# Loading and transposing the first batch by pairs of neighbouring tokens, with products in place of transposes

## The chip, the cores and the metric

The kernel runs on one core of one Trainium2 chip. The metric is device time in microseconds (us) of one execution of the whole program. Engines are named as in the profile: PE is TensorE (the matrix engine), PEld its weight loads, DVE is VectorE, ACT is ScalarE, POOL is GpSimd, SP is SyncE. SP and ACT each own a DMA queue (in the profile, q1 is SP's and q10 is ACT's), and both queues are served by the same 16 DMA engines.

## The reference

Two blocks are computed, one after the other, on B = 8 batches, H = 8 heads, S = 512 tokens of D = 64 values a head, and Ns = 32 state rows a head:

```
scores = x @ state^T / 8            # (8, 8, 512, 32), softmax over the 32 state rows
xread  = softmax(scores) @ state    # tokens read the state
scores2 = state @ x^T / 8           # softmax over the 512 tokens
sread  = softmax(scores2) @ x       # states read the tokens
rows   = concat(xread, sread) per batch, heads side by side   # (8*544, 512)
h = rows @ w_in ; g = h * erf(softplus(h)) ; out = g @ w_out    # d_ff = 2048
```

The output is (4352, 512) in float32. The weights arrive as 8-byte floats and are converted on the chip by ACT and DVE.

## The kernel before

The second block is 99% of what PE does. Batches 1 to 7 and the state rows go through a Strassen-like scheme of seven products (`hidden7`, `project7`, `store7`; L543 and L650 in the profile). Batch 0 is different: it runs while the weights are still being fetched and converted, with plain products (`first0` L764, `some0`/`project` L600), and its order is written out by hand from `first0(0, 0, g0[0])` on. `in_order` pins that order on PE, DVE, ACT and SP, so an instruction that waits holds up everything behind it on its engine.

The change touches the beginning of batch 0. These are its steps, in order:

- **Loads.** `x_t[0]` is one tile of 128 partitions x (4 chunks, 8 heads, 64 values). Chunk c holds tokens 128c to 128c+127, one token a partition. The four chunks are four DMAs (L112) of 256 KB each, in runs of 64 floats (256 bytes); chunks 0 and 2 go on ACT's queue, 1 and 3 on SP's. Before them each queue carries half of the state of batch 0 (32 KB, L109); behind them SP's queue carries the first weights (L138).
- **`attention0`** works in two halves of two chunks each. `turn(t)` transposes the half (L315): for each chunk (order 1, 0 and then 2, 3) and each pair of heads, one PE transpose of 128 tokens x 128 values into PSUM. `copies(t, xp)` moves the result to SBUF, half of it on ACT (L320) and half on DVE (L321). `score(t)` multiplies by the state (L328). Then come 32x32 block transposes of the scores on DVE (L334), the softmax (`exps`: L342 maximum and L343 difference on DVE, L344 exponential on ACT; `sum_` L347), and `normalise`. In program order: half 0 is turned and copied, the state of batch 0 is transposed (L182, copied by L183), a filler product runs (`warm`, L169), half 0 is scored, half 1 is turned, copied and scored.
- **Later users.** `read_tokens(0, ...)` (L277) multiplies the token softmax by `x_t[0]` some 88 us in, and `put_x(0, ...)` (L675) stores the four tiles of output rows of batch 0.

`warm(n)` issues products of the identity that nobody reads. In the profile one float32 product of the program stands as two PE records, and a transpose as one: the opening `warm(8)` is 16 records, the eight transposes of `turn(0)` are eight.

Of the kernel before, what the change touches and what calls it, by code (L numbers as in the profile page):

```python
# [8 lines left out]
F32 = mybir.dt.float32  # L9
# [7 lines left out]
def kernel(  # L17
# [17 lines left out]
    nc = tc.nc  # L35
    B, H, S, D = x.shape
    Ns = state.shape[2]
    d_model, d_ff = moe_w_in.shape
    P = 128
    NI = H // 2  # L40
    NC = S // P
# [4 lines left out]
    TB = S + Ns  # L46
# [5 lines left out]
    xin = ctx.enter_context(tc.tile_pool(name="xin", bufs=1))  # L52
# [10 lines left out]
    ident = const.tile([P, P], F32, name="ident")  # L63
    make_identity(nc, ident)

    x_t = {}


    def load_x(b):
        t = xin.tile([P, NC, H, D], F32, name="x")  # L70
        for h in range(H):
            nc.sync.dma_start(out=t[:, :, h, :], in_=x[b, h].rearrange("(c p) d -> p c d", p=P))
        x_t[b] = t
# [30 lines left out]


    st = const.tile([P, B, P], F32, name="st")
    x_t[0] = xin.tile([P, NC, H, D], F32, name="x")
    for e in range(2):
        (nc.scalar, nc.sync)[e].dma_start(out=st[:, 0, D * e:D * e + D],  # L109
                                      in_=state[0].rearrange("(i e) n d -> e i n d", e=2)[e])  # L110
    for c in range(NC):
        (nc.scalar, nc.sync)[c % 2].dma_start(  # L112
            out=x_t[0][:, c], in_=x[0, :, P * c:P * c + P].rearrange("h p d -> p h d"))

    def load_st():
        for h in range(H):
# [49 lines left out]
    def warm(n):  # L166

        for _ in range(n):
            last = nc.tensor.matmul(out=spare[:, 0:P], lhsT=ident, rhs=ident, start=True,  # L169
                                    stop=True)  # L170
        return last
# [5 lines left out]
    def states(bs, pool=ps_at, name="at"):  # L177


        ps = pool.tile([P, len(bs), P], F32, name=name)  # L180
        for k, b in enumerate(bs):
            last = nc.tensor.transpose(out=ps[:, k], in_=st[:, b, :], identity=ident)  # L182
        nc.scalar.copy(st[:, bs[0]:bs[-1] + 1, :], ps)  # L183
        return last
# [46 lines left out]
    def normalise(a, z1):  # L231
        nc.vector.tensor_scalar(z1, z1, 1e-9, None, op0=ALU.add)
        nc.vector.reciprocal(z1, z1)
        for e in range(2):
            nc.vector.tensor_tensor(a[:, e], a[:, e], over(z1[:, e]), op=ALU.mult)

    def largest(sc):
        m2 = small.tile([P, 2], F32, name="m2")
        for e in range(2):
            nc.vector.reduce_max(out=m2[:, e:e + 1], in_=sc[:, e], axis=AX.X)  # L240
        nc.vector.tensor_scalar(m2, m2, -scale, None, op0=ALU.mult)
        return m2

    def weigh_tokens(sc, m2, a2):

        z2 = small.tile([P, 2], F32, name="z2")
        for e in range(2):
            nc.scalar.activation(out=a2[:, e], in_=sc[:, e], func=ACTF.Exp, bias=m2[:, e:e + 1],
                                 scale=scale, accum_out=z2[:, e:e + 1])
        return z2  # L250

    def inverse(z):
        nc.vector.tensor_scalar(z, z, 1e-9, None, op0=ALU.add)
        nc.vector.reciprocal(z, z)

    def turn_weights(a2):
        a2T = att.tile([P, 2, NC, P], F32, name="sc")
        for e in range(2):
            ps = ps_at.tile([P, NC, P], F32, name="at")
            for c in range(NC):  # L260
                nc.tensor.transpose(out=ps[:, c, :], in_=a2[:, e, P * c:P * c + P],
                                    identity=ident)
            nc.scalar.copy(a2T[:, e], ps)
        return a2T
# [3 lines left out]
    def read_tokens(b, a2T, z2, pool=ps_at, name="at"):  # L268


        xt = x_t.pop(b)
        sr = pool.tile([P, 2, D], F32, name=name)
        for e in range(2):
            for c in range(NC):
                for i in reversed(range(NI)):
                    q = slice(Ns * i, Ns * i + Ns)
                    nc.tensor.matmul(out=sr[q, e, :], lhsT=a2T[:, e, c, q],  # L277
                                     rhs=xt[:, c, 2 * i + e, :],
                                     start=(c == 0), stop=(c == NC - 1))
        sn = sn_t[b] = const.tile([P, 2, D], F32, name="sn0") if b == 0 else \  # L280
            st[:, b - 1, :].rearrange("p (e d) -> p e d", e=2)
        for e in range(2):
            nc.vector.tensor_scalar(sn[:, e], sr[:, e], z2[:, e:e + 1], None, op0=ALU.mult)
# [8 lines left out]
    def attention0(between):  # L292

        H2 = S // 2
        NB = NC * NI // 2
        xt = x_t[0]
        xT = xin.tile([P, NI, S // Ns, Ns], F32, name="xq").rearrange("p i m n -> p i (m n)")
        both = att.tile([P, NI, S], F32, name="xT")  # L300
        sc = att.tile([P, 2, S], F32, name="sc")
        aT[0] = keep.tile([P, 2, S], F32, name="aT")
        a = both[:, 0:2].rearrange("p e (k n) -> p e k n", n=Ns)
        m1, z1 = (small.tile([P, 2, NC * NI], F32, name=n) for n in ("m1", "z1"))
        cols = [slice(H2 * t, H2 * t + H2) for t in range(2)]
        blocks = [slice(NB * t, NB * t + NB) for t in range(2)]
        over = lambda v: v.unsqueeze(3).to_broadcast([P, 2, NB, Ns])

        def turn(t):
            xp = [ps_o.tile([P, 2, H2], F32, name="o%d" % (2 * t)),  # L310
                  ps_h.tile([P, 2, H2], F32, name="h") if t else
                  ps_o.tile([P, 2, H2], F32, name="o1")]
            for c in ((1, 0), (2, 3))[t]:
                for i in range(NI):
                    nc.tensor.transpose(out=xp[i // 2][:, i % 2, P * (c % 2):P * (c % 2) + P],  # L315
                                        in_=xt[:, c, 2 * i:2 * i + 2, :], identity=ident)
            return xp

        def copies(t, xp):
            nc.scalar.copy(xT[:, 0:2, cols[t]], xp[0])  # L320
            nc.vector.tensor_copy(xT[:, 2:4, cols[t]], xp[1])  # L321

        def score(t):
            s2 = [ps_at.tile([P, S], F32, name="at")[:, 0:H2] for _ in range(2)]
            for i in range(NI):
                for e in range(2):
                    r, q = slice(D * e, D * e + D), slice(Ns * i, Ns * i + Ns)
                    nc.tensor.matmul(out=s2[e][q, :], lhsT=st[r, 0, q], rhs=xT[r, i, cols[t]],  # L328
                                     start=True, stop=True)
            return s2  # L330

        def turn_scores(t, s2):
            for e in range(2):
                nc.vector.transpose(out=both[:, e, cols[t]], in_=s2[e])  # L334

        def copy_scores(t, s2):
            for e in range(2):
                nc.scalar.copy(sc[:, e, cols[t]], s2[e])

        def exps(t):  # L340
            k = blocks[t]
            nc.vector.reduce_max(out=m1[:, :, k], in_=a[:, :, k], axis=AX.X)  # L342
            nc.vector.tensor_tensor(a[:, :, k], a[:, :, k], over(m1[:, :, k]), op=ALU.subtract)  # L343
            nc.scalar.activation(out=a[:, :, k], in_=a[:, :, k], func=ACTF.Exp, scale=scale)  # L344

        def sum_(t):
            nc.vector.reduce_sum(out=z1[:, :, blocks[t]], in_=a[:, :, blocks[t]], axis=AX.X)  # L347

        copies(0, turn(0))
        states(range(1), ps_h, "h")  # L350
        warm(1)
        s0 = score(0)
        xp = turn(1)
        turn_scores(0, s0)
        copy_scores(0, s0)
        copies(1, xp)
        warm(3)
        s1 = score(1)
        exps(0)
        between[0]()  # L360
        turn_scores(1, s1)
        exps(1)
        between[1]()
        copy_scores(1, s1)
        sum_(0)
        between[2]()
        sum_(1)
        between[3]()
        normalise(a, z1)
        for e in range(2):  # L370
            nc.vector.transpose(out=aT[0][:, e], in_=both[:, e])

        def rest():
            a2 = both[:, 2:4]
            m2 = largest(sc)
            yield
            z2 = weigh_tokens(sc, m2, a2)
            inverse(z2)
            yield
            a2T = turn_weights(a2)  # L380
            yield
            read_tokens(0, a2T, z2)
            yield

        return rest()
# [9 lines left out]
    def attention(b, xT=None):  # L395
# [40 lines left out]
        if b + 1 < B:  # L436
            load_x(b + 1)
# [231 lines left out]
        put(0, o1, slice(E2, d_model))  # L669

    def put_x(b, h):
        rows = out[TB * b:TB * b + S].rearrange("(c p) e -> c p e", p=P)

        def go(r, ot, c=slice(0, d_model)):
            nc.sync.dma_start(out=rows[2 * h + r][:, c], in_=ot[:, c])  # L675
        return go
# [388 lines left out]
```

## Time and profile before

| | us |
|---|---|
| median of 4 runs | 732.46 (731.81 to 732.93) |
| the profiled execution, whole | 732.70 |
| its span, first to last instruction | 730.9 |
| outside the span | 1.8 |
| PE busy in the span | 722.5 |
| DVE busy | 524.5 |
| ACT busy | 395.8 |
| start of the first transpose of batch 0 | 6.06 |
| end of the last transpose of batch 0 | 11.36 |
| first product of the second block (L764) | 22.4 |

A row of the timeline gives start, duration, engine, line, operation, output and inputs, shape, and how many; in brackets stands the idle time before it and what ended that. The chain of waits is followed back from the last instruction: each piece has a start, the time it adds to the chain, and what ran. A PE record's duration includes the time in which the result drains, so records overlap; what one costs in a row of many is read from the distance of their starts, or from the chain.

### The profile page before, as it was taken

What the parts mean: (1) busy time and instruction counts of PE and PEld (TensorE: products, weight loads), DVE (VectorE), ACT (ScalarE), POOL (GpSimd) and SP (SyncE); (2) the same over time, 40 slices, a digit from 0 to 9 for tenths busy, and PEclk for the clock granted to TensorE, in tenths of its full rate; (3) what the DMA queues carried; (4) which work ended last, traced back from release to release, by engine and by line L of the source; (5) the groups of instructions that cost most, each with busy time, mean ns of one, the idle gap of its engine ahead of it and who ended that gap; (6) DMA issues with size and microseconds to landing.
All of it is one profiled execution on the core that took longest, in us unless ns stands there. A gap on an engine that the chain in (4) does not pass through costs nothing.

```text
span 730.9 us, 12161 instructions
## 1 busy us (share of the span) xinstructions
PE 722.5 (99%) x5032; PEld 588.3 (80%) x5032; DVE 524.5 (72%) x768; ACT 395.8 (54%) x500; POOL 0.7 (0%) x6
## 2 busy tenths in 40 slices
PE   8999999999999999999999999999999999999998
PEld 7434435889889888988989888988898899999996
DVE  4988887997798677867587669866686656674423
ACT  4898894665556444754455445544575434443340
POOL 0000000000000000000000000000000000000000
PEclk9999999999999999999999999999999999999999
DMA  7577842330152103310061104220111000000001
GB/s 234 172 209 249 224 93 58 87 60 30 19 103 65 48 1 65 81 30 30 1 145 25 34 1 96 57 52 2 42 47 30 30 1 30 1 30 1 30 1 29
DMA packets 139166, 46.40 MB, mean 63 GB/s; under 512 B 126696, under 2 KB 130536, under 8 KB 139112
## 3 DMA queue, kind: packets, MB, share of 16 engines
q1 hardware_dynamic: 136708, 44.88, 24.4%
q10 hardware_dynamic: 2404, 0.75, 0.5%
q8 instruction: 39, 0.64, 0.4%
q14 instruction: 15, 0.12, 0.1%
HBM read 33.03 MB, written 8.91 MB: 57 GB/s over the span
## 4 chain that ended last, share of the span: by engine, by line
PE 90%; ACT 5%; DVE 3%; issue 1%; DMA 1%; SPq 0%; DVEq 0%; ACTq 0%
PE o L650 49%; PE h L543 27%; PE o L600 5%; PE at L457 2%; PE h L764 1%; PE h L457 1%; PE at L197 1%; ACT raw L146 1%; PE at L471 1%; ACT L774 1%; DMA x<-in_x_dram 1%; PE h L277 1%; ACT s L774 1%; ACT w_in L144 0%; PE at L277 0%
## 5 line engine op out<-in xcount | busy, mean ns | idle before, releaser
L650 PE MATMUL o<-w_out,s 128*128 128x256 f32 x480 | 118.0, 380 | 0.0
L650 PE MATMUL o<-raw,hs 128*128 128x256 f32 x480 | 117.3, 382 | 0.0
L550 ACT ACTIVATE s<-hs 128x512 f32<-128x512 f32 x120 | 75.3, 629 | 74.3 <-DVE hs L551 74.0
L650 PE MATMUL o<-w_out,hs 128*128 128x256 f32 x480 | 114.1, 380 | 0.0
L650 PEld LDWEIGHTS o<-raw,hs 128*128 128x128 f32 x480 | 89.9, 190 | 22.6 <-issue 10.9
L551 DVE TENSOR_TENSOR hs<-hs,h 128x512 f32<-128x512 f32 x90 | 61.8, 687 | 62.5 <-PE h L543 62.4
L650 PEld LDWEIGHTS o<-w_out,hs 128*128 128x128 f32 x480 | 90.8, 190 | 16.3 <-issue 4.2
L650 PEld LDWEIGHTS o<-w_out,s 128*128 128x128 f32 x480 | 84.6, 191 | 7.9
L551 DVE TENSOR_TENSOR hs<-s,h 128x512 f32<-128x512 f32 x60 | 41.0, 684 | 67.4 <-PE h L543 67.0
L543 PEld LDWEIGHTS h<-aT,m 128*128 128x128 f32 x672 | 83.8, 192 | 4.3 <-issue 1.4
L543 PE MATMUL h<-aT,m 128*128 128x128 f32 x672 | 84.4, 275 | 0.0
L595 DVE TENSOR_TENSOR s<-s,hs 128x2048 f32<-128x2048 f32 (+1 forms) x31 | 68.7, 2218 | 20.4 <-ACT s L593 20.4
L554 ACT COPY s<-h 128x512 f32<-128x512 f32 x29 | 17.0, 585 | 107.7 <-PE h L543 107.7
L600 PE MATMUL o<-w_out,s 128*128 128x512 f32 x128 | 59.1, 600 | 0.6 <-DVE s L777 0.5
L543 PE MATMUL h<-sy,sx 128*128 128x128 f32 x448 | 59.4, 275 | 0.0
L543 PEld LDWEIGHTS h<-sy,sx 128*128 128x128 f32 x448 | 56.7, 192 | 2.0 <-issue 0.5
L593 ACT ACTIVATE s<-s 128x2048 f32<-128x2048 f32 x30 | 57.4, 1912 | 0.3
L559 ACT COPY hs<-h 128x512 f32<-128x512 f32 x29 | 16.9, 584 | 74.8 <-PE h L543 74.8
L650 PE MATMUL o<-raw,s 128*128 128x256 f32 x240 | 56.8, 379 | 0.0
L600 PEld LDWEIGHTS o<-w_out,s 128*128 128x128 f32 x128 | 23.1, 190 | 31.1 <-issue 25.8
L650 PEld LDWEIGHTS o<-raw,s 128*128 128x128 f32 x240 | 43.5, 190 | 4.7
L550 ACT ACT_TABLE_LOAD x31 | 39.8, 1283 | 0.5
(139 smaller groups left out, 917.1 us busy)
## 6 DMA issues: line engine op xcount, KB each, us to landing
raw<-in_moe_w_in_dram SPq DMA_DIRECT2D x8, 1024.0 KB, 5.3
raw<-in_moe_w_out_dram SPq DMA_DIRECT2D x8, 1024.0 KB, 4.7
xq<-in_x_dram SPq DMA_DIRECT2D x112, 64.0 KB, 2.1
x<-in_x_dram SPq DMA_DIRECT2D x56, 128.0 KB, 2.7
out_dram<-ot SPq DMA_DIRECT2D x18, 256.0 KB, 2.0
sc<-xT SPq DMA_DIRECT2D x112, 32.0 KB, 1.9
out_dram<-ot SPq DMA_DIRECT2D x28, 128.0 KB, 1.7
x<-in_x_dram SPq DMA_DIRECT2D x2, 256.0 KB, 5.3
```

The costliest lines, as they stand in the source:

```text
L146: lambda: nc.scalar.activation(out=lo, in_=lo, func=ACTF.Copy, scale=2.0 ** -29)], \
L457: nc.tensor.matmul(out=ps[k][e][q, :], lhsT=st[r, b, q], rhs=w_in[r, 2 * g:2 * g + 2, i, :], start=True, stop=True)
L543: last = nc.tensor.matmul(out=bank[:, q], lhsT=lhsT, rhs=rhs, start=(first and i == 0 and k == 0), stop=(i == GF - 1 and k == len(ops) - 1 ...
L550: nc.scalar.activation(out=s[:, k], in_=hs[:, k], func=ACTF.Softplus)
L551: add = lambda o, x, y: nc.vector.tensor_tensor(o, x, y, op=ALU.add)
L554: copy(m1, p)
L559: copy(c11, p)
L593: nc.scalar.activation(out=s, in_=s, func=ACTF.Erf)
L595: nc.vector.tensor_tensor(s[:, k], s[:, k], hs[:, k], op=ALU.mult)
L600: nc.tensor.matmul(out=acc[r], lhsT=gT[:, i, P * r:P * r + P], rhs=w_out[:, GF * g + i, :], start=(g == 0 and i == 0), stop=(g == NG - 1 a ...
L650: nc.tensor.matmul(out=acc[bank][:, E2 * c:E2 * c + E2], lhsT=lhs[:, i, :], rhs=rhs[:, g, i, :], start=(first and i == 0 and c == 0), stop ...
L774: nc.scalar.activation(out=gT[0][:, ks], in_=gT[0][:, ks], func=ACTF.Erf)
```

## The change

The tile of `x` of batch 0 gets the order (heads, chunks, values) in each partition, and "chunk" c of partition p now means token 4p + c. The load is again four DMAs of 256 KB: half t (chunks 2t and 2t + 1, that is two neighbouring tokens of each partition) and four heads each. Two neighbouring tokens of a head lie side by side in memory, so a run is now 512 bytes. ACT's queue carries heads 0 to 3 of both halves, SP's heads 4 to 7. `turn` no longer issues a transpose for a pair of heads but two products with the identity, one for a head: 128 tokens x 64 values as the stationary operand, 128 columns of the identity moving, into partitions 0 to 63 or 64 to 127 of the same PSUM region. `put_x(0, ...)` stores row 4p + c of the output from partition p of tile c. Everything else, the order of the other instructions on all engines included, is as before.

```diff
-    x_t[0] = xin.tile([P, NC, H, D], F32, name="x")
+    x_t[0] = xin.tile([P, H, NC, D], F32, name="x").rearrange("p h c d -> p c h d")
...
-    for c in range(NC):
-        (nc.scalar, nc.sync)[c % 2].dma_start(
-            out=x_t[0][:, c], in_=x[0, :, P * c:P * c + P].rearrange("h p d -> p h d"))
+    for t in range(2):
+        for k in range(2):
+            c, h = slice(2 * t, 2 * t + 2), slice(4 * k, 4 * k + 4)
+            (nc.scalar, nc.sync)[k].dma_start(
+                out=x_t[0][:, c, h].rearrange("p c h d -> p h c d"),
+                in_=x[0, h].rearrange("h (p c) d -> p h c d", c=NC)[:, :, c])
...
             for c in ((1, 0), (2, 3))[t]:
                 for i in range(NI):
-                    nc.tensor.transpose(out=xp[i // 2][:, i % 2, P * (c % 2):P * (c % 2) + P],
-                                        in_=xt[:, c, 2 * i:2 * i + 2, :], identity=ident)
+                    for e in range(2):
+                        nc.tensor.matmul(
+                            out=xp[i // 2][D * e:D * e + D, i % 2, P * (c % 2):P * (c % 2) + P],
+                            lhsT=xt[:, c, 2 * i + e, :], rhs=ident, start=True, stop=True)
...
-        rows = out[TB * b:TB * b + S].rearrange("(c p) e -> c p e", p=P)
+        rows = out[TB * b:TB * b + S].rearrange("(p c) e -> c p e" if b == 0 else
+                                                "(c p) e -> c p e", p=P)
```

## The prediction

> **What bounds the kernel now.** I read the page first, for what bounds the whole:
>
> ```profile
> span 730.9 us, 12161 instructions
> PE 722.5 (99%) x5032; PEld 588.3 (80%) x5032; DVE 524.5 (72%) x768; ACT 395.8 (54%) x500; POOL 0.7 (0%) x6
> ```
>
> PE is at work nearly always, but in the opening much of that is filler. So I read the chain of waits over the first 60 us:
>
> ```profile
> 1.54 4.47 DMA x<-in_x_dram
> 6.02 0.04 issue
> 6.06 2.22 PE o L315 x8
> 8.28 0.21 PE h L182
> 8.49 0.43 PE o L169 x2
> 8.92 1.22 PE at L328 x16
> 10.14 0.55 PE o L315 x2
> 10.69 0.22 PE h L315 x2
> 10.91 0.22 PE o L315 x2
> 11.12 0.23 PE h L315 x2
> 11.36 0.02 issue
> 11.38 0.69 DVE xq L321
> 12.07 0.60 DVE m L342
> ...
> 15.56 0.63 ACT xT L344
> ...
> 22.57 3.47 PE h L764 x8
> ```
>
> Every piece that the change touches is on the chain: the load of x, both turns (L315), the score of half 0 between them (L328), and the DVE copy behind the last transpose (L321). From there it goes through DVE, ACT and PE to the end, and the load of x is the only DMA on it. Later work waits for computation and not for a clock of its own, so I take a shift of the copy at 11.38 to reach the end in full.
>
> Third, the timeline, for what a turn waits for and costs, and for a product with column groups:
>
> ```profile
> 1.35 3.78 PE L169 MATMUL o<-ident 128*128 128x128 f32 x16 [1.35 <-POOL ident masks.py:199]
> 6.06 2.22 PE L315 MATMUL o<-ident,x 128*128 128x128 f32 x8 [0.93 <-DMA x<-in_x_dram]
> 7.16 0.72 PEld L315 LDWEIGHTS o<-ident,x 128*128 128x128 f32 x4 [0.38 <-DMA x<-in_x_dram]
> 87.63 1.10 PE L277 MATMUL at<-x,sc 128*32 128x64 f32 x64
> ```
>
> `warm(8)` is 16 records, two for a float32 product; the eight transposes of half 0 are eight, one each. PE waits twice: until 6.06 for chunk 1 (SP's queue), until 7.16 for chunk 0 (ACT's). L277's 32 products go to four groups of 32 columns, and its 64 records take 1.03 us of the chain.
>
> Fourth, the DMA view, asked for 4 to 5, 6 to 7 and 10 to 12 us:
>
> ```profile
> DMA packets 1139, 0.29 MB, mean 288 GB/s; under 512 B 1139, under 2 KB 1139, under 8 KB 1139
> DMA packets 857, 0.22 MB, mean 217 GB/s; under 512 B 857, under 2 KB 857, under 8 KB 857
> DMA packets 416, 0.82 MB, mean 410 GB/s; under 512 B 16, under 2 KB 16, under 8 KB 416
> ```
>
> With 256-byte packets (x) both queues together move 217 to 288 GB/s; with 2 KB packets (weights) 410.
>
> **The change part by part.** A difference of 0.2% (1.46 us) is about what a measurement of this kernel tells from none.
>
> *Loads.* The first product now needs ACT's DMA, the later one, and the other 15 stand behind it; half 0 starts when both DMAs have landed. ACT's packets of x start in number near 3.85 us (53 between 3.8 and 4.0, 28 in the 0.4 us before). The landing at 7.16 is 3.3 us later, of which 1.1 lie behind the last packet (SP's chunk 1: last packet near 4.95, PE released at 6.06). So 2.2 us are transfer. The trace has no 512-byte packets. By the packet time of 16 engines, 256 B at 217 GB/s is 18.9 ns and 2 KB at 410 GB/s is 79.9 ns; on the line between them 512 B is 27.6 ns, or 297 GB/s, 1.37 times the rate. 2.2 / 1.37 = 1.6, so the landing is at 3.85 + 1.6 + 1.1 = 6.55: **-0.6 us**. Ends: no faster (7.16); the full 410/217 = 1.89 times, with 0.3 us less to issue since half as many packets are described: 5.8. I take the line because 512 is far nearer to 256 than to 2048.
>
> The Trainium skill, "DMA: Bandwidth & Descriptors", Specifications, puts the smallest transfer for line rate at 512 B and the fabric's ceiling at 435 GB/s. By it 2.2 us would become 2.2 x 217 / 435 = 1.1 and the landing 6.05, half a microsecond better than my line; no row here shows it.
>
> *Turn of half 0.* Eight transposes become 16 products, 32 records of 128 columns. Before the clock of PE rises a record costs 0.22 us (four transposes from 7.16 to about 8.04). One after the other that is 7.0 us; with two column groups at once 3.5. L277 shows such groups at work: 64 records of 64 columns in 1.03 us are 16.1 ns each, and 64 columns alone would cost 55.7 ns by the 0.111 us of 128 columns (L543: 16 records in 1.78 us), so 3.46 run at once where 4 could. For two groups that is 1.73 to 2; records twice as long carry less overhead, and I take 1.9: 3.7 us. Behind the landing of the second DMA there were four transposes, 0.9 us. So **+2.8 us**, ends +2.6 and +6.1. PE reaches 10.25, and with the same 0.25 us of drain the DVE copy of half 0 starts near 10.5 instead of 8.3.
>
> *Behind it.* L182, L183 and the filler keep their 0.64 us, and the score starts near 11.15. The records of L315 fall from 0.22 to 0.11 us apart at about 10.5; I take it that PE's clock rises at the same time after the change. Then the score of half 0 runs at the pace that half 1 has now (0.82 us against 1.22): **-0.4 us**, end +0.2 if the clock rises later.
>
> The Trainium skill, "TensorE: Matmul & The Clock Gate", Part 1, has PE at half clock until a window of about 3.4 us was busy, with windows that run free. It agrees with the step from 0.22 to 0.11; its windows could fall differently in another run, which would move the sum by some tenths.
>
> *Turn of half 1.* Its data has long landed. 32 records at 0.111 / 1.9 are 1.87 us, with 0.1 of drain 1.95, against 1.22 (10.14 to 11.36): **+0.7 us**, ends +0.65 and +2.4.
>
> The same page's Terms call the transpose mode four times as fast for FP32. Here warm() and L315 show two records against one, so a factor of two; by the page half 1 would be 3.7 us and the sum about 5 us worse. The rows decide.
>
> *At nothing.* The DVE block transposes of the scores of half 0 stay ahead of the copy of half 1 and end well before it (10.97 against 11.38 now). Weight loads are of 64 columns and run beside the other group's products, as L277's do (0.94 us of loads within 1.03); if they did not, the turns would be the serial ones below. The stores at about 130 us keep 2 KB packets and counts; only the next user of `ot` would wait, and a store lands in 2.2 us. L277 reads 64 floats in a row as before. Weights follow x on SP's queue and come earlier, but ACT takes the first of them at 13.96 behind its own work, so nothing is gained.
>
> **Sum.** -0.6 + 2.8 - 0.4 + 0.7 = +2.5 us at the copy at 11.38, and all that follows. On the profiled execution: span 733.4, whole 735.2. It lay 0.24 above the median, so against the median 732.46 + 2.5 = 735.0.
>
> **The rivals.**
>
> *The early landing pays the products back (not slower).* If x lands by 5.8, the pause of PE behind the filler shrinks from 0.93 to 0.7 us and the work from 1.35 on is nearly unbroken; I price the case that the clock then rises at 7.0 instead of 10.5, after 5.6 us, where now it rises 4.4 us after the pause. Then 1.2 of the 3.7 us are cold, the rest takes 1.27, half 0 ends near 8.5, the score runs from 9.0 to 9.8 and half 1 is turned at 11.8: +0.4, 732.9, not to be told from before. It decides from a landing at about 5.9. For it speaks the 410 GB/s of large packets; against it, that ACT's packets start at 3.85 and share the engines with SP's second DMA.
>
> *No two products at once.* If the groups of 64 columns run in turn, half 0 takes 3.9 us cold and 1.6 warm, to 12.05, the score ends near 13.6, half 1 takes 3.65: 17.3, +5.9, 738.4. Against it speaks L277, whose groups do overlap.
>
> *Faster.* Even a landing at 5.0 with the clock up at 7.0 gives some -0.2. To be faster by 1.5 us the turn would have to cost no more than the transposes, for which no row speaks.
>
> **How the numbers follow.** My forecast 0.67, with its own range 733.9 (landing 5.8 without the early clock, pairing 2) to 736.2 (landing 7.16, pairing 1.73); the early landing 0.20; in turn 0.08; faster 0.05. The range leaves out the serial case, the faster one and the lower edge of the early landing: 732.6 to 736.8. Slower by over 0.2% is above 733.9: 0.65 of the forecast and the serial case, 0.73; within: 0.22; faster: 0.05.
>
> **What would show it.** The load: first product of x near 6.55 and only one wait for x. The products: 64 records on the turn's line, of form 128*64, with half 0 taking about 3.7 us and half 1 1.9. The chain: DVE's copy of half 1 starting near 13.9, and the distance from there to the end as before. A first product before 5.9, records 0.11 us apart before 10 us, or a later stage that swallows the shift would make it wrong.

## The result and the profile after

The changed kernel takes 733.32 us in the median of 31 runs (732.38 to 735.03), the kernel before 732.44 in the median of 51 (731.08 to 734.58). The ratio is 1.0017, 95% interval 1.0011 to 1.0023: slower by a fifth of a percent, about 1.2 us (the medians are 0.9 apart). I had forecast 735.0, 2.5 us more. The profiled execution of the changed kernel took 734.94 us; from the profiled one of before I had worked out 735.2. So the sum fits the profile that it was made for, and is at least twice too large for the typical run. Why, is the subject of what follows.

The page of the changed kernel, first the whole:

```profile
span 733.1 us, 12257 instructions
PE 724.1 (99%) x5080; PEld 590.3 (81%) x5080; DVE 524.5 (72%) x768; ACT 395.9 (54%) x500; POOL 0.7 (0%) x6
```

48 more PE records are 16 transposes of one record replaced by 32 products of two. Its timeline at the opening (start, duration, engine, line, operation, tile, shape, count, and the wait before):

```profile
6.58 3.65 PE L321 MATMUL o<-ident,x 128*64 128x128 f32 x32 [1.45 <-DMA x<-in_x_dram]
10.28 0.69 DVE L328 COPY xq<-o 128x512 f32<-128x512 f32 x1 [10.28 <-PE o L321]
10.84 0.82 PE L335 MATMUL at<-xq,st 64*32 64x256 f32 x16
11.59 0.66 PE L321 MATMUL o<-ident,x 128*64 128x128 f32 x8
13.60 0.69 DVE L328 COPY xq<-h 128x512 f32<-128x512 f32 x1 [1.11 <-PE h L321]
```

One wait for x, until 6.58 (forecast 6.55); half 0 in 3.65 us (forecast 3.7); the score of half 0 in 0.82; DVE's copy of half 1 at 13.60 (forecast near 13.9) instead of 11.38. The DMA view, for 4 to 5 and 5 to 6 us:

```profile
DMA packets 691, 0.34 MB, mean 343 GB/s; under 512 B 21, under 2 KB 691, under 8 KB 691
DMA packets 640, 0.32 MB, mean 318 GB/s; under 512 B 20, under 2 KB 640, under 8 KB 640
```

The 512-byte packets move 343 and 318 GB/s, where the 256-byte packets of before moved 288 and 235 in the same two stretches: 1.19 and 1.35 times as much, forecast 1.37.

The profile follows the chain of waits of the changed kernel back only to 28.80 us, so the passage of the shift is read from a piece that both chains have. In the chain of the changed kernel:

```profile
56.50 7.13 PE o L607 x16
```

The same 16 products stand in the chain of before as

```profile
54.24 7.13 PE o L600 x16
```

They are 2.26 us apart, and the spans are 2.2 us apart. Nothing later swallowed any of it.

### The profile page after: what moved, and what is told of

Its sections match the earlier page's. It is cut to its first block, busy times and chain, and to the rows that moved or that the text cites. A ratio compares the mean times of both kernels' runs of the same rounds, so it can differ in the third digit from the quotient of the medians.

```text
span 733.1 us, 12257 instructions
## 1 busy us (share of the span) xinstructions
PE 724.1 (99%) x5080; PEld 590.3 (81%) x5080; DVE 524.5 (72%) x768; ACT 395.9 (54%) x500; POOL 0.7 (0%) x6
## 4 chain that ended last, share of the span: by engine, by line
PE 90%; DVE 3%; ACT 2%; issue 1%; DVEq 0%; ACTq 0%
PE o L657 49%; PE h L550 27%; PE o L607 7%; PE at L464 2%; PE h L464 1%; PE h L772 1%; PE at L202 1%; PE at L478 1%; PE h L282 1%; DVE s L785 0%; PE at L282 0%; DVE hs L779 0%; ACT L782 0%; DVE w_out L153 0%; DVE xT L396 0%
```

## Experiments

Two theories were open after the first comparison. CLOCK says that PE's records are 0.22 us apart at first and 0.11 later, that the moment of that fall differs from run to run, and that the two profiles had it after half 0, which most executions do not. LANDING says that the runs differ because x lands at different times, and that a turn always costs the same. The times of the changed kernel speak for some switch: of 31 runs 19 lie between 732.38 and 733.58, 12 between 734.45 and 735.03, none between.

The experiments were timed in three series, each with runs of the kernel before beside them, and that kernel's own median was 732.31, 731.93 and 732.32 us in them. Where two runs of different series are compared, their ratios to the kernel before say more than their medians.

**The changed kernel a second time**, for another profile.

> The changed kernel itself, for the profile of another execution. Theory CLOCK: the profiled execution of the changed kernel had PE's clock low until about 10.1 us; in other executions it rises before x lands, records of half 0 then start 0.11 us apart, and the whole is 732.4 to 733.6 us instead of 734.5 to 735.0. Rival LANDING: x lands at different times, and half 0 always takes about 3.65 us. If this execution takes 734.5 or more, both expect the old profile; if it takes less, CLOCK expects a first product at 6.6 us and half 0 in 1.9 us, LANDING a first product at 4.5 to 5.5 us.

733.16 us, span 731.4, in the lower group. Its timeline:

```profile
6.53 1.97 PE L321 MATMUL o<-ident,x 128*64 128x128 f32 x32 [1.52 <-DMA x<-in_x_dram]
8.54 0.69 DVE L328 COPY xq<-o 128x512 f32<-128x512 f32 x1 [8.54 <-PE o L321]
9.86 0.66 PE L321 MATMUL o<-ident,x 128*64 128x128 f32 x8
11.87 0.69 DVE L328 COPY xq<-h 128x512 f32<-128x512 f32 x1 [1.11 <-PE h L321]
```

x lands at the same time, 6.53 against 6.58, but the same 32 records take 1.97 us instead of 3.65. DVE's copy of half 1 is 1.73 us earlier, and so is the end (span 731.4 against 733.1). So the difference between these two executions is PE's pace and not the landing. At 1.97 us a record costs 0.062, not 0.111 as one of its width alone, so two column groups do run at once.

**The kernel before a second time.**

> The kernel before itself, for the profile of another execution. Theory CLOCK: the time goes with the moment at which PE's records fall from 0.22 to 0.11 us apart: near 731.2 us if that is before 6 us, near 732.7 if near 10.5, near 733.5 if later. Rival: no relation.

731.60 us, span 729.8. The first four transposes, from 5.68, still start 0.21 us apart; the next four, behind the second landing at 6.81, run at the faster pace, 0.11 apart once they are under way:

```profile
5.68 1.79 PE L315 MATMUL o<-ident,x 128*128 128x128 f32 x8 [0.54 <-DMA x<-in_x_dram]
6.81 0.42 PEld L315 LDWEIGHTS o<-ident,x 128*128 128x128 f32 x4 [0.41 <-DMA x<-in_x_dram]
8.09 0.80 PE L328 MATMUL at<-xq,st 64*32 64x256 f32 x16 [0.29 <-ACT st L183]
```

The score of half 0 takes 0.80 us here and took 1.29 in the first profile, and the copy of half 1 starts at 10.34, not 11.38. The landing differs too (5.68 against 6.06). It also moves in the changed kernel: in the five traces that turn ACT's heads first, PE gets x at 5.72 to 6.58. So x's landing can account for a part of the spread, some 0.9 us, and PE's pace for 1.7.

**Filling the pause.** If the clock follows PE's activity, filler up to the landing of x should bring its rise ahead of half 0 in every run. The edit is the same in both kernels, with 11 for the changed one, 10 for the one before:

```diff
     for _ in range(3):
         fetch()
-    warm(8)
+    warm(11)
```

> The changed kernel with 11 filler products ahead of the first turn instead of 8, which at the low clock end near 6.5 us, when x lands. Theory CLOCK: PE does not pause, its clock has risen by about 7 us in every execution, the upper group of times (734.4 to 735.0) is gone and the median is 732.6 us. Rival LANDING: filler has nothing to do with it, two groups as before, median 733.3 us.

> The kernel before with 10 filler products ahead of the first turn instead of 8, which at the low clock end at 6.07 us, when the first x lands. Theory CLOCK: the clock has risen before the first transpose; four transposes from 6.06 take 0.45 us, PE waits for chunk 0 until about 7.1, half 0 ends near 7.8, DVE's copy of half 1 starts near 10.3 instead of 11.38; median 731.4 us with a narrow spread. The change at equal clock then costs 732.9 - 731.4 = 1.5 us. Rival: the filler only helps the changed kernel, whose products are longer; median 732.3 us as before and the change at equal clock costs 0.6.

The changed kernel: 732.91 us (732.71 to 733.70, 11 runs); the upper group is gone. The kernel before: 731.50 (731.15 to 732.69, 11 runs), six runs up to 731.5 and five from 732.17, so the median is as expected and the spread is not as narrow. The filled changed kernel's timeline:

```profile
6.14 1.97 PE L321 MATMUL o<-ident,x 128*64 128x128 f32 x32 [0.47 <-DMA x<-in_x_dram]
8.16 0.69 DVE L328 COPY xq<-o 128x512 f32<-128x512 f32 x1 [8.16 <-PE o L321]
9.47 0.66 PE L321 MATMUL o<-ident,x 128*64 128x128 f32 x8
11.49 0.69 DVE L328 COPY xq<-h 128x512 f32<-128x512 f32 x1 [1.11 <-PE h L321]
```

and that of the filled kernel before:

```profile
6.12 1.19 PE L315 MATMUL o<-ident,x 128*128 128x128 f32 x8 [0.39 <-DMA x<-in_x_dram]
7.35 0.69 DVE L321 COPY xq<-o 128x512 f32<-128x512 f32 x1 [7.35 <-PE o L315]
8.78 0.44 PE L315 MATMUL o<-ident,x 128*128 128x128 f32 x2
9.91 0.69 DVE L321 COPY xq<-h 128x512 f32<-128x512 f32 x1 [0.35 <-PE h L315]
```

In this pair PE gets its first x at the same time and the clock has risen in both, so it prices the change most cleanly. From the first transpose or product to the copy of half 0 it is 1.23 us before and 2.02 after (+0.79), from there to the turn of half 1 1.43 and 1.31 (-0.12), to the copy of half 1 1.13 and 2.02 (+0.89): together with 0.02 of landing +1.58, and the spans (729.4, 731.0) are 1.6 apart. The medians are 1.41 apart, but of different series; by the two ratios to the kernel before (1.0013 and 0.9999) it is 1.0.

**Emptying the opening.** The opposite edit, `warm(8)` to `warm(1)`, lets PE idle until x lands.

> The changed kernel with 1 filler product ahead of the first turn instead of 8: PE does nothing from about 1.8 us until x lands. Theory CLOCK: the clock rises in no execution before half 0 is well under way, all times lie in the upper group or above it, 734.4 to 736 us, median 735.0. Rival (the spread has another source, such as the landing of x): two groups as in the changed kernel, median 733.3.

> The kernel before with 1 filler product instead of 8. Theory CLOCK: all of half 0 and its score at the low clock, and in some executions the turn of half 1 as well: 732.6 to 734.2 us, median 733.2; the change at a low clock costs 735.0 - 733.2 = 1.8 to 2.3 us. Rival (the spread has another source): median 732.3 us, 731.1 to 734.

The changed kernel: 734.38 us (734.29 to 735.04, 5 runs), the lower group is gone. The kernel before: 733.17 (731.98 to 734.54, 11 runs). Timelines, the changed kernel first:

```profile
6.02 3.69 PE L321 MATMUL o<-ident,x 128*64 128x128 f32 x32 [3.87 <-DMA x<-in_x_dram]
```

and the kernel before:

```profile
5.89 2.12 PE L315 MATMUL o<-ident,x 128*128 128x128 f32 x8 [3.74 <-DMA x<-in_x_dram]
8.57 1.29 PE L328 MATMUL at<-xq,st 64*32 64x256 f32 x16
```

Here x lands early (6.02) and half 0 is slow all the same. The change costs 1.27 us at the copy of half 1 (13.08 against 11.81) and 1.21 in the medians (1.5 by the ratios), under the 1.8 to 2.3 that I had expected and less than in the first two profiles, since the kernel before now turns half 1 at the low pace too (9.80 to 11.81), and the changed one, whose products kept PE busy longer, does not (11.06 to 13.08, with a score of 0.67 us). The two edits with `warm` empty one group and then the other while the load of x is left alone.

The traces settle it. Besides the instructions each keeps records of the granted clock. The views show a clock of 1.00 from the start, because nothing is recorded before the first of these; that first record, of the full clock, begins somewhere in the opening, and where PE is at work then, its records fall from 0.21 to 0.11 us apart at that moment (it stands in the last table below). With 8 filler products it begins anywhere from 4.3 to 10.5 us (seven traces), with 10 to 12 at 4.7 to 6.6 (four), with 1 at 10.0 and 11.9. CLOCK is shown.

**The products alone**: load, layout and stores of before, `turn` of after.

```diff
                 for i in range(NI):
-                    nc.tensor.transpose(out=xp[i // 2][:, i % 2, P * (c % 2):P * (c % 2) + P],
-                                        in_=xt[:, c, 2 * i:2 * i + 2, :], identity=ident)
+                    for e in range(2):
+                        nc.tensor.matmul(
+                            out=xp[i // 2][D * e:D * e + D, i % 2, P * (c % 2):P * (c % 2) + P],
+                            lhsT=xt[:, c, 2 * i + e, :], rhs=ident, start=True, stop=True)
```

> Load, layout and stores of before (256-byte runs, four DMAs by chunks), but a product a head instead of a transpose for two heads. My accounting: chunk 1 is turned while chunk 0 is still coming (6.06 to 7.9 us with a low clock, chunk 0 to 9.75), so half 0 ends 0.4 us earlier than in the changed kernel although x lands later: median 732.9 us, 0.5 above before and 0.4 below the changed kernel. Rival: the 512-byte load pays about 0.6 us of the products back, so without it the time is 0.6 above the changed kernel, 733.9 us.

733.20 us (11 runs: eight from 732.58 to 733.49, three from 734.15 to 734.83). That is the changed kernel's time (ratio 1.0015, 95% interval 1.0006 to 1.0023, against 1.0017), neither 0.4 below nor 0.6 above. Its timeline:

```profile
6.43 1.97 PE L316 MATMUL o<-ident,x 128*64 128x128 f32 x32 [1.64 <-DMA x<-in_x_dram]
```

Chunk 1 released PE at 6.43, and the products of chunk 0 followed without a wait, so with the risen clock half 0 ended 0.1 us earlier than with the new load (11.77 against 11.87). The load by pairs moves its bytes faster, but no gain from it shows in these times, which leave some tenths of a microsecond open: half 0 of before may start on the first DMA that lands, half 0 of after needs the later one from its first product. As far as these runs can tell, all of the change's cost is in the products.

**The turn in the order of the loads.** If that is so, starting with SP's heads, which land first, should give the load its worth:

```diff
-            for c in ((1, 0), (2, 3))[t]:
-                for i in range(NI):
+            for ks in (2, 3), (0, 1):
+                for c, i in [(c, i) for c in ((1, 0), (2, 3))[t] for i in ks]:
```

> The changed kernel with the turns in the order of the loads: heads 4 to 7 of both chunks (SP's queue) before heads 0 to 3 (ACT's). My accounting: SP's DMA lands near 5.95 us and its 8 products run while ACT's is still coming, so half 0 ends 0.4 to 0.6 us earlier: median 732.8 us. Rival: the second DMA's landing is not what half 0 waits for, or the order costs as much elsewhere (DVE's copy now comes first and ACT's last): no change, 733.3 us.

733.94 us in the median, a miss: four runs at 731.71 to 732.38, eight at 733.87 to 734.41. Each group lies about 0.6 below that of the changed kernel, as my accounting has it, but more runs fell into the upper one (8 of 12 against 12 of 31, which may be chance). With 10 filler products the groups are out of the way:

> The changed kernel with the turns in the order of the loads and 10 filler products. With a risen clock heads 4 to 7 are turned while ACT's DMA is still coming, half 0 ends near 7.65 instead of 8.16 in the filled changed kernel: median 732.3 us, no upper group. Rival: the order moves the wait to ACT's copy, which then comes after DVE's; no gain, 732.9 us. By neither is it faster than the kernel before.

732.32 us (731.90 to 732.85, 11 runs), a single group, so the high median of the one without filler was a matter of the groups. It is 0.6 below the filled changed kernel, by the ratios too, but these are of different series and their intervals overlap (1.0004, 0.9995 to 1.0013, against 1.0013, 1.0004 to 1.0022): a gain is likely, not shown. Nor can it be told from the kernel before. The rival had a point, too: the gain at DVE's copy of half 1 (11.04 here) does not reach the end in full. The chain of waits, which runs over that copy in the kernel before, runs here over PE, through three filler products (L174) and the score of half 1 (L335), to DVE's block transpose of that score, which waits for it here and does not in the changed kernel:

```profile
11.87 0.86 PE o L174 x6
12.73 0.70 PE at L335 x16
13.44 0.77 DVE xT L341 x2
```

The timeline has the wait:

```profile
13.42 0.78 DVE L341 STREAM_TRANSPOSE xT<-at 128x256 f32<-128x256 f32 x2 [0.36 <-PE at L335]
```

**Without taking turns.** The four products into partitions 0 to 63 of a chunk first, then the four into 64 to 127:

```diff
-                for i in range(NI):
-                    for e in range(2):
+                for e in range(2):
+                    for i in range(NI):
```

> The changed kernel with the products of a chunk in another order: the four into partitions 0 to 63 first, then the four into 64 to 127, instead of taking turns. My reading: two products run at once because neighbours in the queue go to different column groups; without that 32 records at a risen clock take up to 3.5 us instead of 1.97 and the time rises by up to 3 us, to 734.5 to 736.5. Rival: order does not matter to the overlap (or the 0.06 us a record has another reason, such as the half width of the weights): half 0 in 1.97 us at a risen clock, median 733.3 us as the changed kernel.

734.96 us (733.74 to 735.98, 6 runs), 1.6 above the changed kernel in the medians, 1.1 by the ratios (1.0032 against 1.0017). In its timeline half 0 is

```profile
5.72 2.77 PE L321 MATMUL o<-ident,x 128*64 128x128 f32 x32 [0.59 <-DMA x<-in_x_dram]
```

but its first few records ran before the clock rose, at 6.2 us. The clean comparison is half 1, all of it at the risen clock: from 9.84 to the copy at 12.45 it takes 2.61 us against 2.01. The order in the queue matters to the overlap, though part of it remains: with no overlap the records of a half would take 3.55.

**A longer filler in the kernel before**: `warm(12)`.

> The kernel before with 12 filler products instead of 8 or 10: at the low clock they end at 7.0 us, at a clock that rises on the way before 6.1. Theory CLOCK: PE never pauses, the clock has risen by 7 us at the latest; the 732.2 to 732.7 us of the 10-product version become 731.5 to 732.2, median 731.4 us, faster than the kernel before by 0.5 to 1.0 us. Rival: the longer filler holds back the first transposes as often as it helps; median 731.9 to 732.4 us.

731.87 us (731.08 to 734.31, 12 runs), ratio 0.9999 (0.9989 to 1.0008): a miss, where 731.4 was expected and the rival had 731.9 to 732.4. Its profiled execution is the shortest of all (span 729.3, copy of half 1 at 9.88), but other runs are late. No filler made a kernel that is measurably faster than the one before.

**All profiles side by side.** Start of the record of the full clock, start of DVE's copy of half 1, and the span:

| profiled kernel | full clock from, us | copy of half 1, us | span, us | span less copy |
|---|---|---|---|---|
| before | 10.5 | 11.38 | 730.9 | 719.5 |
| before, again | 6.6 | 10.34 | 729.8 | 719.5 |
| before, filled (10) | 5.3 | 9.91 | 729.4 | 719.5 |
| before, filled (12) | 6.0 | 9.88 | 729.3 | 719.4 |
| before, bare | 11.9 | 11.81 | 731.4 | 719.6 |
| changed | 10.1 | 13.60 | 733.1 | 719.5 |
| changed, again | 4.7 | 11.87 | 731.4 | 719.5 |
| changed, filled (11) | 4.7 | 11.49 | 731.0 | 719.5 |
| changed, bare | 10.0 | 13.08 | 732.6 | 719.5 |
| products alone | 4.3 | 11.77 | 731.3 | 719.5 |
| changed, grouped | 6.2 | 12.45 | 731.9 | 719.5 |
| changed, order of the loads | 6.8 | 10.59 | 730.5 | 719.9 |
| the same, filled (10) | 6.6 | 11.04 | 731.0 | 720.0 |

Whatever moves the copy moves the end by as much, to a tenth of a microsecond, in the first eleven. In the last two DVE's copy comes so early that PE's work sets the pace behind it, and about 0.4 us of the gain at that copy is lost in the wait shown above. Counted from DVE's block transpose of the score of half 1, where the two ways meet, the rest is 717.5 to 717.6 us in all thirteen.

## Why the prediction was right, and where its size was not

- **The bound.** That the copy of half 1 at 11.38 sets the end, and that later work passes a shift on in full, is shown by the table for all kernels but the two in the order of the loads.
- **The sum against its own profile.** Forecast +2.5 at the copy, found +2.22. By terms: landing -0.6 and half 0 +2.8, together +2.2, found +1.96 (from 6.06 and 8.32 to 6.58 and 10.28); what lies between -0.4, found -0.44; half 1 +0.7, found +0.70. Two column groups run 1.8 at once (0.062 us against 0.111), taken at 1.9. That both profiles had the clock rise just after 10 us is chance: to judge by the times, only 12 of 31 runs of the changed kernel are like that.
- **The step that failed** is "I take it that PE's clock rises at the same time after the change", and with it the last line of the sum, which carried the difference of two such executions over to the medians. The term mis-sized by it is the turn of half 0. Counted as in the sum, from the second landing to DVE's copy, it was put at +2.8; it is +2.5 in the first two profiles (1.16 and 3.70 us) and +1.3 in the filled pair (0.70 and 2.02), where the clock has risen by then, which to judge by the times is so in 19 of 31 runs of the changed kernel. The landing of -0.6 held: -0.58 in the first two profiles, -0.5 in the filled pair (6.65 and 6.14). With the clock risen throughout the change costs 1.0 (ratios) to 1.6 us (spans), with an empty opening 1.2 to 1.5; over all runs it is 1.2 by the ratio.
- **The chances.** I gave 0.73 to slower by over 0.2%; 1.0017 falls just within that bound, which had 0.22. The median of 733.32 lies below the forecast's own range (733.9 to 736.2) and inside the whole one only because the early-landing rival had drawn its lower edge down to 732.6; that is in part luck. This rival had the right mechanism, an early clock that makes the products cheap, but hung it on the landing: in the second profile x lands at 6.53, as late as I took it to, and the clock has risen at 4.7 all the same. With that one of my signs of being wrong came true, records at the fast pace before 10 us. (The -0.2 that I gave for a landing at 5.0 comes to about 0 by the steps of that rival.) I had read the clock of one execution as a property of the kernel, though the text names another run's clock as free to differ, "some tenths"; it is 1.7 us between two profiles of one program.
- **The serial rival** is excluded by 1.97 us for 32 records; what a worse order costs, the grouped run shows.
- **At nothing.** The stores by strided rows and the reads of the token tile 88 us in cost nothing that shows: span less copy is that of before.

The Trainium skill, "TensorE: Matmul & The Clock Gate", Part 1, has PE at half clock until a window of about 3.4 us was busy, the windows running free of the program. The runs agree: two paces a factor of 1.9 apart (0.213 and 0.110 us between transposes), an early rise with filler up to the landing, a late one without, and a moment that differs between executions of the same program (10.1 and 4.7 us). A step of that length shows too: the stretch at the full clock lasts 720.2, 723.6 or 727.0 us in the thirteen traces, whole steps of 3.4 us apart. How much of a window must be busy is shown by no run here. The clock row of the views reads 1.0 throughout the opening, so with them alone this switch has to be read from the distance of the records.

## What to carry to other kernels

Price a stage near the start of a kernel at both paces of PE, and compare kernels in more than one profile: here two profiles of one program differ by more than the change is worth. A faster transfer can gain nothing where the first instruction behind it needs the last transfer of a group instead of the first (733.20 us with the old load, 733.32 with the new); matching the order of use to the order of landing probably gained some tenths here, and left the rest in a wait for PE. A float32 product with the identity is two records where a transpose is one, and taking turns between two column groups gives back most of that, not all, and best where neighbours in the queue alternate.

## What the runs showed that was not expected

A filler of products decides by its length in which pace a stage 5 us later runs: in the changed kernel 1, 8 and 11 of them give 734.38, 733.32 and 732.91 us in the median, and 1.0036, 1.0017 and 1.0013 as ratios to the kernel before. And 512-byte packets moved 318 to 343 GB/s here, where the straight line had 297. The line was drawn from the slowest stretch of the 256-byte packets (217); in the stretches compared above their gain was smaller than forecast. The landing came out as forecast even so: PE gets the second DMA at 6.65 to 7.16 in four traces of the old load and at 5.72 to 6.58 in five of the new.
